# Four layers of sliding-window attention and Fourier mixing on one core: split weights kept in DRAM, residual rows loaded ahead, one late chunk regrouped, fill casts on GpSimd

## The chip, the core and the metric

The kernel runs on one core of a Trainium2 chip (trn2). The metric is the device time of one execution in microseconds (us); times given as a median are over several executions. Engines are named as the profile has them: PE (TensorE, the matmuls), PEld (its weight loads), DVE (VectorE), ACT (ScalarE), POOL (GpSimd), SP (SyncE, whose queue issues the DMAs).

## What is computed

The input `x` has S = 2048 rows of D = 640. Four layers run in a row, attention, Fourier, attention, Fourier, each as `x = x + layer(layernorm(x))`, with the same weights in both layers of a kind.

```python
def _A_ref(x, wqkv, wo):                       # H = 32 heads of Dh = 20, W = 256
    qkv = (lambda x, *d: x.transpose(*d))((x @ wqkv).reshape(B, S, 3, H, Dh), 2, 0, 3, 1, 4)
    q, k, v = qkv[0], qkv[1], qkv[2]
    scores = jnp.einsum("bhqd,bhkd->bhqk", q, k) * (Dh ** -0.5)
    mask = (idx[:, None] - idx[None, :] >= 0) & (idx[:, None] - idx[None, :] < W)
    scores = jnp.where(mask[None, None], scores, -1e9)
    o = jnp.einsum("bhqk,bhkd->bhqd", _softmax(scores, axis=-1), v)
    return o.transpose(0, 2, 1, 3).reshape(B, S, D) @ wo

def _B_ref(x, dft_seq_re, dft_seq_im, dft_hid_re, dft_hid_im):
    a = jnp.einsum("bsd,ed->bse", x, dft_hid_re)
    b = jnp.einsum("bsd,ed->bse", x, dft_hid_im)
    return jnp.einsum("ts,bse->bte", dft_seq_re, a) - jnp.einsum("ts,bse->bte", dft_seq_im, b)
```

## The kernel before

**Arithmetic.** Each fp32 operand of a large matmul is cut into two parts, hi (its cast to f32r) and lo (the operand minus hi), and each product is three matmuls (`product3`, L251; two half-array products at once in `lockstep`, L273). The cut is a cast on ACT and a subtraction on DVE or POOL (`split`, L242 and L248; as queued jobs `cut_job`, L235, and `sub_job`, L227, which halves a row tile on POOL).

**Stages of an attention layer** (`attention`, L372). `before_heads` normalises and transposes x and makes v and the first q/k chunks. `heads` (L631) has 8 quads of 4 heads and 16 steps a quad. A step makes a score block in one order (L656) and its row maximum on DVE (L661), sends the maxima, as `mt` (ACT, L672), by DMA into a row of `qp` (L674), makes the transposed scores with that row in the product (L684), takes the exponential on ACT (L694), masks it on POOL (L700, L704), and multiplies it with v (L719). So a row of maxima that is late holds L684 of the quad behind it. `after_heads` ends the layer, and interleaves its end with the start of the Fourier layer.

**What fills PE between the steps.** Three generators, taken up in this order by `fill`: `project` (L587) makes q/k chunks 2 to 9 of 128 columns, in sets of four 512-row blocks or, for the last two chunks, in the order `LAST` of two blocks each; `partials` (L1007) multiplies the first three of five 128-row chunks of the heads' output with `wo` and adds the residual rows (L1030); `late` (L1077) adds the last two chunks, the rest of the layer's output (L1117, L1123) and the next norm. A chunk is a regrouping of the 640 rows of the output by `CHUNKS` (rectangles of heads x columns), and each rectangle costs two DMAs, one of the output (L907) and one of the softmax denominators' reciprocals (L910). Scaling (L940; L923 after the heads) and the cut come behind them.

**What sets the order.** Engines run in the order of the program. [...] `tick` runs twice a step: it runs what was posted for now (`post`), takes one request for output chunks (`asks`) if a raw buffer is free (`room`), and takes one job from each of the lanes `act`, `dve` and `pool` (`job`).

**Weights before.** `load_chunk` (L514) loads a raw q/k weight chunk, `cut_chunk` (L520) cuts it by jobs on ACT and POOL, in both attention layers. `prepare(2)`, run at `LAST[2]`, asks for three raw `wo` chunks (`load_early`, L983), cut on ACT and DVE (key "ew"), beside the first output chunks; `poll_late` (L1055) loads the other two in the last quad, cut on POOL (key "lw"). `prepare(4)`, when `project` is at its end, loads the first four residual row blocks (L1005).

**A q/k result** is copied from PSUM by ACT (L563), cast on ACT (L571, a job of the lane `act`), subtracted on POOL in two jobs, and stored one tick later to `qk_d` (L542), from which `pack` loads the next quad's q and k (L619). **The late chunks** 3 and 4 both hold heads of the last quads; `late_load` (L1046) loads both, four rectangles or eight DMAs a block, when the last quad's part is stored.

## Time and profile before

| what | us |
|---|---|
| median of 3 runs (2234.83 to 2236.5) | 2236.22 |
| the profiled execution | 2236.0 |
| its span, first to last instruction | 2234.3 |
| PE busy | 2137.6 |
| DVE busy | 1605.3 |
| ACT busy | 1159.8 |
| POOL busy | 968.1 |

The profiled execution is 1.7 us longer than its span, and 0.2 us below the median. In rows of the timeline the columns are the start, the duration, the engine (SPq is SP's DMA issue), the line of the kernel and the operation, the tile written and the tiles read, and the count; in brackets stands the idle time of the engine before it and what ended it. Rows of groups have busy time, the mean in ns, and the idle time before. The two attention layers have their head stages at about 125 to 560 us and 1230 to 1660 us, and the Fourier layers lie between and behind. Such lines are quoted where the prediction uses them.

### The profile page before, as it was taken

Reading aid. Unit: us, or ns where it says so; the run is one execution under the profiler, and the core shown is the slowest. Engines: PE = TensorE matmul, PEld = TensorE weight load, DVE = VectorE, ACT = ScalarE, POOL = GpSimd, SP = SyncE. Lnnn points to the kernel's source line nnn. Section 1 sums busy time; section 2 is a strip of 40 time slices with the busy share of each in tenths; the row PEclk is TensorE's granted clock in tenths of the full one; section 3 lists DMA queues with packets and bytes.
Section 4 is the critical chain, followed back from the end, with each engine's and each line's share of the span. In section 5 each row is a group of like instructions: output and inputs, shape, how many; then the busy total and the mean of one; then the engine's idle time right before and its main releaser. Section 6 shows DMA issues by size and latency. Waiting matters only on the chain. (4 is left out here: it accounts for less than half of the span.)

```text
span 2234.3 us, 49112 instructions
## 1 busy us (share of the span) xinstructions
PE 2137.6 (96%) x17944; PEld 1787.5 (80%) x17944; DVE 1605.3 (72%) x3925; ACT 1159.8 (52%) x2161; POOL 968.1 (43%) x1572
## 2 busy tenths in 40 slices
PE   7999999898989999999999999998988999999999
PEld 7987777676868888889999777766777688888899
DVE  6357777685897868786661677776858978687776
ACT  2127776566554545452431477775665545455432
POOL 3036666775513223222330466667755132342324
PEclk9999999999999999999999999999999999999999
DMA  5545666774535354665646466667645354546653
GB/s 188 179 155 183 191 185 195 216 208 128 182 124 184 125 184 135 208 202 192 207 143 187 149 192 183 192 199 229 187 146 165 118 175 139 181 129 228 209 170 129
DMA packets 220498, 392.13 MB, mean 176 GB/s; under 512 B 39520, under 2 KB 86112, under 8 KB 220256
## 3 DMA queue, kind: packets, MB, share of 16 engines
q1 hardware_dynamic: 220256, 388.98, 55.3%
q8 instruction: 142, 2.33, 0.4%
q14 instruction: 100, 0.82, 0.1%
HBM read 273.94 MB, written 113.77 MB: 174 GB/s over the span
## 5 line engine op out<-in xcount | busy, mean ns | idle before, releaser
L661 DVE CUSTOM_DVE_ANT_0 banks<-banks,mask 128x384 f32<-128x384 f32 (+2 forms) x1024 | 527.8, 557 | 160.7 <-PE banks L656 135.5
L694 ACT ACTIVATE pt<-banks 128x768 f32<-128x768 f32 (+2 forms) x512 | 393.6, 770 | 177.2 <-PE banks L684 81.1
L700 POOL TENSOR_SCALAR_AFFINE_SELECT pt<-pt 128x256 f32<-128x256 f32 x512 | 210.8, 412 | 251.1 <-ACT pt L694 223.0
L273 PE MATMUL banks<-big,wc 64*128 64x512 f32 x1920 | 273.6, 396 | 0.4 <-DVE pt L459 0.4
L684 PE MATMUL banks<-qp,kp 61*128 61x384 f32 (+2 forms) x1024 | 209.9, 381 | 34.4 <-DVE mc L661 23.5
L656 PE MATMUL banks<-kp,qp 60*128 60x384 f32 (+2 forms) x1024 | 210.6, 351 | 11.4 <-ACT pt L694 10.5
L719 PE MATMUL banks<-pt,vq 128*32 128x128 f32 x5760 | 211.3, 278 | 1.6 <-ACT pt L694 1.6
L273 PEld LDWEIGHTS banks<-big,wc 64*128 64x128 f32 x1920 | 186.6, 186 | 25.0 <-ACT x L563 4.2
L684 PEld LDWEIGHTS banks<-qp,kp 61*128 61x128 f32 x1024 | 108.7, 185 | 97.4 <-DVE mc L661 62.1
L704 POOL TENSOR_SCALAR_AFFINE_SELECT pt<-pt 128x256 f32<-128x256 f32 x448 | 182.9, 408 | 0.0
L719 PEld LDWEIGHTS banks<-pt,vq 128*32 128x32 f32 x5760 | 142.2, 110 | 49.0 <-issue 36.1
L242 ACT ACTIVATE c<-pt 128x512 fp32r<-128x512 f32 x150 | 93.7, 626 | 160.8 <-POOL pt L1333 52.9
L242 ACT ACTIVATE qp<-pt 128x512 fp32r<-128x512 f32 (+1 forms) x195 | 119.8, 624 | 108.5 <-DVE pt L1347 51.0
L248 DVE TENSOR_TENSOR c<-pt,c 128x512 fp32r<-128x512 f32 x150 | 123.6, 826 | 54.6 <-ACT c L242 51.8
L656 PEld LDWEIGHTS banks<-kp,qp 60*128 60x128 f32 x1024 | 124.8, 187 | 44.0 <-ACT pt L694 27.1
L1413 PE MATMUL banks<-qp,big 128*128 128x512 f32 x630 | 154.5, 398 | 4.4 <-ACT qp L242 1.7
L248 DVE TENSOR_TENSOR qp<-pt,qp 128x512 fp32r<-128x512 f32 (+1 forms) x191 | 148.4, 785 | 12.6 <-ACT qp L242 9.9
L1346 POOL TENSOR_TENSOR pt<-pt,pt 128x512 f32<-128x512 f32 x34 | 50.3, 1481 | 236.3 <-DMA pt<-c 180.0
L661 DVE DVE_READ_ACCUMULATOR2_ANT mc<- 128x1 f32 x1024 | 145.2, 142 | 0.0
L1413 PEld LDWEIGHTS banks<-qp,big 128*128 128x128 f32 x630 | 120.3, 193 | 31.1 <-ACT qp L242 2.6
L1413 PE MATMUL banks<-qp,xc 128*128 128x512 f32 x480 | 117.3, 390 | 0.8 <-DVE xc L248 0.8
L227 POOL TENSOR_TENSOR c<-x,c 128x256 fp32r<-128x256 f32 x128 | 94.1, 741 | 44.1 <-ACT c L571 41.9
(240 smaller groups left out, 4474.3 us busy)
## 6 DMA issues: line engine op xcount, KB each, us to landing
pt<-c SPq DMA_DIRECT2D x188, 512.0 KB
qk_d<-c SPq DMA_DIRECT2D x80, 512.0 KB
kp<-qk_d SPq DMA_DIRECT2D x384, 80.0 KB
qp<-qk_d SPq DMA_DIRECT2D x384, 80.0 KB
kp<-u_d SPq DMA_DIRECT2D x32, 640.0 KB
o_d<-ou SPq DMA_DIRECT2D x64, 256.0 KB
x_d<-x SPq DMA_DIRECT2D x48, 320.0 KB
v_d<-pt SPq DMA_DIRECT2D x16, 768.0 KB
```

The lines of the kernel that those rows point to most:

```text
L227: eng.tensor_tensor(out=lo[..., c], in0=src[..., c], in1=hi[..., c].bitcast(F32), op=OP.subtract)
L242: nc.scalar.activation(hi, src, AF.Copy, scale=-1.0 if neg else 1.0)
L248: (eng or nc.vector).tensor_tensor(out=lo, in0=src, in1=hi.bitcast(F32), op=OP.subtract)
L273: self.nc.tensor.matmul(ps[a], x[r], y[r], start=half + i == 0, stop=half == 1 and i == n - 1, skip_group_check=True)
L656: nc.tensor.matmul(p, qp[quad % 2][b:b + 60, z, qb * P:(qb + 1) * P], kp[quad % 2][b:b + 60, z, k0 * P:(qb + 1) * P], start=True, stop=True)
L661: nc.vector.tensor_tensor_reduce(out=p, in0=p, in1=self.mask[:, 384 - n * P:], scale=1.0, scalar=NEG, op0=OP.add, op1=OP.max, accum_out=mc ...
L684: nc.tensor.matmul(self.banks[:, banks[e], :n * P], kp[quad % 2][b:b + 61, z, kb * P:(kb + 1) * P], qp[quad % 2][b:b + 61, z, kb * P:(kb + ...
L694: nc.scalar.activation(pt[quad, kb][:, 2 * z:2 * z + 2, :n * P], self.banks[:, b0:b1 + 1, :n * P], AF.Exp, scale=SCALE)
L700: nc.gpsimd.affine_select(out=t[:, :, 0:P], in_=t[:, :, 0:P], pattern=[[0, 2], [1, P]], compare_op=OP.is_ge, fill=0.0, base=0, channel_mul ...
L704: nc.gpsimd.affine_select(out=t[:, :, 256:384], in_=t[:, :, 256:384], pattern=[[0, 2], [-1, P]], compare_op=OP.is_gt, fill=0.0, base=0, ch ...
L719: nc.tensor.matmul(self.banks[32 * h:32 * h + 32, bank, :P], vq[:, 96 * (kb % 4) + 21 * h:96 * (kb % 4) + 21 * h + 32], t[:, h, (qb - kb) ...
L1413: nc.tensor.matmul(self.banks[:, bk, :], p, b[q], start=start and m == 0, stop=stop and last and m == 2, skip_group_check=True)
```

## The change

1. **q/k weights.** In the first attention layer a chunk is cut as before, and both parts are also stored to DRAM (`wq_d`, 640 KB a chunk). In the second (`fresh` is false) `cut_chunk` is one DMA of the parts into the tile, and there is no raw load, cast or subtraction.
2. **Output weights.** In the first layer `keep_wo` takes `wo` in ten halves of 320 columns, one every six steps: load, cast on ACT, subtraction on POOL, two stores to `wo_d`. Both layers then load parts: six DMAs of 320 KB in `prepare(2)`, four in `poll_late`. The cuts "ew" and "lw" go.
3. **Residual rows.** The 128-row blocks 0 and 1 are loaded into a tile of the weights' ring ("wc") at `LAST[3]`; `prepare(4)` loads blocks 2 and 3 only; the add of `partials` reads them from there.
4. **Late chunks.** Chunk 3 becomes heads 20 to 27, columns 0 to 15, one rectangle without a head of the last quad. Chunk 4 is heads 16 to 27, columns 16 to 19, and heads 28 to 31: two rectangles. The 512-row blocks 0 and 1 of chunk 3 are loaded at the start of the last quad (`late_first`) and worked on POOL while the heads run; its blocks 2 and 3, and chunk 4, stay after it.
5. **Casts of q/k results** move from ACT to POOL (`tensor_copy`, lane `pool`), the store comes three ticks after the subtraction instead of one, and `asks` wants one more free buffer. The last quad's reciprocals and their stores come a tick later.

The diff, without the helper arguments that follow from it:

```diff
 CHUNKS = (((0, 16, 0, 8),), ((0, 16, 8, 16),), ((0, 16, 16, 20), (16, 20, 0, 16)),
-          ((16, 20, 16, 20), (20, 28, 0, 14)), ((20, 28, 14, 20), (28, 32, 0, 20)))
+          ((20, 28, 0, 16),), ((16, 28, 16, 20), (28, 32, 0, 20)))
...
         self.od = dram.tile([H, 32, S], F32, name="o_d")
+        self.wod = dram.tile([2, KC, P, D], F32, name="wo_d")
+        self.wqd = dram.tile([NCH, P, 2 * D], F32, name="wq_d")
         self.rd = dram.tile([NSB, H, 512], F32, name="r_d")
...
         self.xn = {}
-        self.ready, self.hid = 0, False
+        self.ready, self.hid, self.fresh = 0, False, True
         self.slot = None
...
                 f()
-        if self.asks and self.room(2):
+        if self.asks and self.room(3):
             self.asks.popleft()()
...
     def load_chunk(self, c):
-        if c < NCH:
+        if c < NCH and self.fresh:
             raw, free = self.hold()
...
     def cut_chunk(self, c):
-        if c < NCH:
-            raw, free = self.turn.pop(("wraw", c))
-            w = self.work.tile([P, 2, KC, P], F32R, name="wc", tag="wc")
-            raw = raw.rearrange("p (k c) -> p k c", c=P)
-            self.turn["w", c] = w
-            if self.slot is None:
-                self.split(w[:, 0], w[:, 1], raw, eng=self.nc.gpsimd if c < 2 else None)
-                free()
-                return
-            for ks, done in ((slice(0, 3), None), (slice(3, KC), free)):
-                self.cut_job("pool", ("w", c), w[:, 0, ks], w[:, 1, ks], raw[:, ks], done)
+        if c >= NCH:
+            return
+        w = self.work.tile([P, 2, KC, P], F32R, name="wc", tag="wc")
+        self.turn["w", c] = w
+        flat = w.rearrange("p l k c -> p (l k c)").bitcast(F32)
+        if not self.fresh:
+            self.nc.sync.dma_start(flat, self.wqd[c])
+            return
+        raw, free = self.turn.pop(("wraw", c))
+        raw = raw.rearrange("p (k c) -> p k c", c=P)
...
+        def keep():
+            self.nc.sync.dma_start(self.wqd[c], flat)
+        if self.slot is None:
+            self.split(w[:, 0], w[:, 1], raw, eng=self.nc.gpsimd if c < 2 else None)
+            free()
+            keep()
+            return
...
+        def done():
+            free()
+            self.post(3, keep)
+        for ks, f in ((slice(0, 3), None), (slice(3, KC), done)):
+            self.cut_job("pool", ("w", c), w[:, 0, ks], w[:, 1, ks], raw[:, ks], f)
...
+    def keep_wo(self, i):
...
+        if i == 0:
+            self.wt = [self.slot_tile(f"rr{n}", 512, dt)[:, :320] for n, dt in enumerate((F32R, F32R, F32))]
+        if i == 2 * KC:
+            self.rr = [self.slot_tile(f"rr{n}", 512, F32) for n in range(3)]
+            return
+        k, cs = i // 2, slice(i % 2 * 320, i % 2 * 320 + 320)
+        hi, lo, raw = self.wt
+        self.nc.sync.dma_start(raw, self.a["wo"][:, k, cs])
...
+        def keep():
+            for n, t in enumerate((hi, lo)):
+                self.nc.sync.dma_start(self.wod[n, k, :, cs], t.bitcast(F32))
+        self.post(5, lambda: self.cut_job("pool", ("wo", i), hi, lo, raw, lambda: self.post(2, keep)))
...
                 if self.c_live == 3:
-                    self.post(1, lambda: self.job("act", key, lead))
+                    self.post(1, lambda: self.job("pool", key, lead))
                     return
...
                 st = self.work.tile([P, 2, 512], F32R, name="c", tag="c", bufs=3)
-                self.nc.scalar.activation(st[:, 0, :], r, AF.Copy)
-                self.sub_job("pool", key, st[:, 1, :], r, st[:, 0, :], lambda: (free(), self.post(1, lambda: store(st))))
+                self.nc.gpsimd.tensor_copy(st[:, 0, :], r)
+                self.sub_job("pool", key, st[:, 1, :], r, st[:, 0, :], lambda: (free(), self.post(3, lambda: store(st))))
...
                 self.packable.add((c, sb))
-            self.job("act", key, lead)
+            self.job("pool", key, lead)
         for r in self.lockstep(sets):
...
                 self.prepare(2)
+            if (c, sbs) == LAST[3]:
+                self.y_first = cuts(self.work.tile([P, 2 * D], F32, name="y", tag="wc"), D)
+                for t, y in enumerate(self.y_first):
+                    self.nc.sync.dma_start(y, self.xsrc[t * P:(t + 1) * P, :])
             yield from self.pieces(c, sbs, "m")
...
             cols = slice(bk * 512, (bk + 1) * 512)
-            at = (2, 9, 11) if quad < NQ - 1 else (1, 5, 6)
+            at = (2, 9, 11) if quad < NQ - 1 else (1, 6, 7)
             self.post(at[0], lambda: nc.sync.dma_start(sm, ou[0:P:32, :]))
...
                 f()
+            if self.fresh and step >= 0 and step % 6 == 2 and step // 6 <= 2 * KC:
+                self.keep_wo(step // 6)
             s, t, v = step + LEAD, step, step - 1
...
         key = "o", sb, k
-        lane, n, wait = ("pool", 2, 7) if k < EARLY else ("dve", 1, 4)
-        eng = nc.gpsimd if k < EARLY else nc.vector
+        busy = self.step + LEAD < 16 * NQ
+        lane, n = ("pool", 2) if busy else ("dve", 1)
+        wait = 7 if busy else 4
+        eng = nc.gpsimd if busy else nc.vector
...
             self.early_o = [dict(zip(ks, pairs(oc[:6]))), dict(zip(ks, pairs(oc[6:])))]
-            self.ask(0, self.load_early)
+            for k in ks:
+                self.load_wo(k, self.early_w[k])
+            self.ask(0)
             self.ask(1)
...
             self.take_big(2, F32)
-            self.load_y(range(AHEAD_X))
...
-    def load_early(self, k):
-        raw, free = self.hold()
-        self.nc.sync.dma_start(raw, self.a["wo"][:, k, :])
-        self.early_cut += 1
...
-        def cut():
-            self.early_cut -= 1
-            self.cut_job("dve", "ew", *self.early_w[k], raw, free)
-        self.post(4, cut)
...
-    def ask(self, sb, also=None):
+            self.load_y(range(2, AHEAD_X))
...
+    def load_wo(self, k, w):
+        for n in range(2):
+            self.nc.sync.dma_start(w[n].bitcast(F32), self.wod[n, k])
...
+    def ask(self, sb):
         o = self.early_o[sb % 2]
...
                 self.load_o(o, sb, k)
-            if also:
-                self.asks.append(lambda k=k: also(k))
             self.asks.append(one)
...
             assert b1 == b0 + 1
-            y = y.rearrange("p (f c) -> p f c", f=2)
-            nc.vector.tensor_tensor(out=y, in0=self.banks[:, b0:b0 + 2, :320], in1=y, op=OP.add)
+            x, y = [v.rearrange("p (f c) -> p f c", f=2) for v in (self.y_first[t] if t < 2 else y, y)]
+            nc.vector.tensor_tensor(out=y, in0=self.banks[:, b0:b0 + 2, :320], in1=x, op=OP.add)
             self.part_t = t + 1
...
         t = self.part_t
-        return t == NB or t % 4 or not (self.early_o[t // 4 % 2]["left"] or self.early_cut or
-                                        any("ew" == j[1] for q in self.lanes.values() for j in q))
+        return t == NB or t % 4 or not (self.early_o[t // 4 % 2]["left"])
...
+    def late_raws(self, sb):
+        p, c = [cuts(t, 512) for t in self.pt], self.late_c
+        return (cuts(c[2], 512), [c[0][:, :512], c[1][:, :512]], [p[0][2], p[1][2]], [p[2][2], None])[sb]
...
+    def late_first(self, sb):
+        o = self.late_pre[sb] = self.late_set(sb)
+        self.load_o(o, sb, EARLY, self.late_raws(sb)[0], self.vq[0] if sb == 3 else None)
...
     def late_load(self):
-        self.flush("lw")
         sb = len(self.late_o)
-        o = self.late_set(sb)
+        if sb not in self.late_pre:
+            self.late_first(sb)
+        o = self.late_pre[sb]
         self.late_o.append(o)
-        p, c = [cuts(t, 512) for t in self.pt], self.late_c
-        raws = (cuts(c[2], 512), [c[0][:, :512], c[1][:, :512]], [p[0][2], p[1][2]], [p[2][2], None])[sb]
-        for k in range(EARLY, KC):
-            self.load_o(o, sb, k, raws[k - EARLY], self.vq[k - EARLY] if sb == 3 else None)
+        self.load_o(o, sb, EARLY + 1, self.late_raws(sb)[1], self.vq[1] if sb == 3 else None)
...
             for k in range(EARLY, KC):
-                raw = self.late_c[k - EARLY][:, :D]
-                self.nc.sync.dma_start(raw, self.a["wo"][:, k, :])
-                self.post(4, lambda k=k, raw=raw: self.cut_job("pool", "lw", *self.late_w[k - EARLY], raw))
+                self.load_wo(k, self.late_w[k - EARLY])
+        if n in (1, 4):
+            self.late_first(n // 4)
         if n == 4:
...
         self.hid = True
+        self.fresh = False
```

6 lines of the change are left out of this document (2 added, 4 removed).

## The prediction

> **What bounds the kernel now.** I read the head of the page first, then the list of what TensorE waited for, then each long wait in the timeline. Columns of the page: busy us, share of the span, instructions.
>
> ```profile
> span 2234.3 us, 49112 instructions
> PE 2137.6 (96%) x17944; PEld 1787.5 (80%) x17944; DVE 1605.3 (72%) x3925; ACT 1159.8 (52%) x2161; POOL 968.1 (43%) x1572
> ```
>
> TensorE (PE) is busy 96% of the span, so the idle time left in the whole kernel is 2234.3 − 2137.6 = 96.7 us. The change leaves the order of instructions on PE as it is: each of its matmuls stays, in the same place. All that it can win is idle time of PE and the slow clock that follows idle time. Next, what ended those waits (us in total, times, longest):
>
> ```profile
> PE banks L684 <- DVE mc L661: 23.5, 39, 5.0
> PE banks L656 <- ACT pt L694: 10.5, 27, 1.3
> PE banks L255 <- DVE x L1123: 7.2, 4, 3.7
> PE banks L255 <- DVE kp L227: 6.6, 2, 3.4
> PE banks L684 <- DMA qp<-mt: 5.8, 2, 3.0
> ```
>
> A few long waits carry most of it. The timeline of PE has them one by one, four in each attention layer (start, duration; in brackets the idle time before it and what ended it):
>
> ```profile
> 419.72 0.44 PE L684 MATMUL banks<-qp,kp 61*128 61x384 f32 x2 [2.78 <-DMA qp<-mt]
> 438.37 0.58 PE L684 MATMUL banks<-qp,kp 61*128 61x256 f32 x2 [4.61 <-DVE mc L661]
> 556.29 0.56 PE L255 MATMUL banks<-qp,kp 128*128 128x320 f32 x2 [3.37 <-DVE kp L227]
> 574.50 0.56 PE L255 MATMUL banks<-qp,kp 128*128 128x320 f32 x1 [2.24 <-DVE x L1123]
> ...
> 1527.05 0.69 PE L684 MATMUL banks<-qp,kp 61*128 61x384 f32 x2 [3.04 <-DMA qp<-mt]
> 1545.85 0.58 PE L684 MATMUL banks<-qp,kp 61*128 61x256 f32 x2 [4.96 <-DVE mc L661]
> 1663.46 0.90 PE L255 MATMUL banks<-qp,kp 128*128 128x320 f32 x2 [3.22 <-DVE kp L227]
> 1683.02 0.85 PE L255 MATMUL banks<-qp,kp 128*128 128x320 f32 x4 [3.71 <-DVE x L1123]
> ```
>
> I call the four kinds, in this order, the **mt**, **y**, **late 1** and **late 2** stall. They sum to 13.0 + 14.93 = 27.9 us. They cost more than their own length. Stretches behind two of them, and one of the undisturbed head stage (stretch, length, then busy us of PE, PEld, DVE, ACT, POOL, granted PE clock, DMA share, GB/s):
>
> ```profile
> 574.70:578.00 3.30, 3.30 (x13) 3.30 (x14) 2.96 (x9) 0.96 (x3) 1.93 (x2) 0.50 0.90 274
> 1544.00:1550.80 6.80, 4.95 (x42) 4.35 (x46) 4.26 (x14) 1.19 (x2) 1.63 (x4) 0.50 0.87 271
> ...
> 206.00:262.00 56.00, 54.17 (x750) 40.15 (x746) 44.57 (x167) 42.72 (x78) 35.66 (x86) 1.00 0.58 180
> ```
>
> After a stall PE runs at clock 0.50 for some 3.3 us, or 6.8 us after the longest. A stretch that is full of matmuls at half clock loses half its length: 3.3/2 = 1.65 us, and 4.95/2 = 2.5 us of the long one. I count 1.65 for each stall but that one. So eight stalls hold 27.9 + 7 × 1.65 + 2.5 = 42 us, 1.9% of the span: the most that the change can win from them. In the undisturbed head stage PE has 54.17 of 56 us; little is to be had there.
>
> [...]
>
> **The change, part by part.**
>
> *Residual rows ahead (y).* How the vector engine and the queue of SyncE stand at the stall:
>
> ```profile
> 1540.24 2.27 SPq L1005 DMA_DIRECT2D big<-x_d  x5
> ```
>
> ```profile
> 1539.44 0.14 DVE L661 DVE_READ_ACCUMULATOR2_ANT mc<- 128x1 f32 x1
> 1544.44 0.82 DVE L1030 TENSOR_TENSOR big<-banks,big 128x640 f32<-128x640 f32 x1 [4.86 <-DMA big<-x_d]
> 1553.16 0.82 DVE L1030 TENSOR_TENSOR big<-banks,big 128x640 f32<-128x640 f32 x1 [0.20 <-PE banks L684]
> ```
>
> DVE stands 4.86 us at L1030 for a load that was issued at 1540.24 only; the row maxima that PE needs stand behind it. The changed kernel loads rows 0 and 1 one filler earlier, into a tile that is free when the filler LAST[2] ends, and L1030 reads them there. Rows 2 and 3 keep the old place, but the second L1030 came 8.7 us after the first, and the third is again later, while the load took 4.2 us. So this stall goes whole: 4.61 + 4.96 + 1.65 + 2.5 = **−13.7 us**. What is late next on DVE is a matmul result (0.20 us above). Two more 320 KB DMAs stand earlier on SyncE's queue; that is in the mt term.
>
> *One late chunk out of the last quad (late 1, late 2).*
>
> ```profile
> 1648.16 0.66 SPq L907 DMA_DIRECT2D cr<-o_d  x1
> ...
> 1653.58 0.76 SPq L910 DMA_DIRECT2D rr<-r_d  x1
> ...
> 1671.08 0.67 SPq L910 DMA_DIRECT2D rr<-r_d  x1
> ...
> 1673.72 1.37 SPq L910 DMA_DIRECT2D rr<-r_d  x1
> ```
>
> ```profile
> 1658.12 1.30 DVE L940 TENSOR_TENSOR cr<-cr,rr 128x512 f32<-128x512 f32 x2 [0.34 <-DMA r_d<-rc]
> ...
> 1662.72 1.28 DVE L227 TENSOR_TENSOR kp<-cr,kp 128x512 fp32r<-128x512 f32 x2
> ```
>
> ```profile
> 569.65 0.69 DVE L923 TENSOR_TENSOR pt<-pt,rr 128x512 f32<-128x512 f32 x1 [2.15 <-DMA rr<-r_d]
> ...
> 1676.29 0.69 DVE L923 TENSOR_TENSOR pt<-pt,rr 128x512 f32<-128x512 f32 x1 [2.34 <-DMA rr<-r_d]
> 1678.18 0.69 DVE L923 TENSOR_TENSOR pt<-pt,rr 128x512 f32<-128x512 f32 x1 [1.19 <-DMA rr<-r_d]
> ```
>
> Late 1: eight small DMAs, two scales (1.30 us) and two subtractions (1.28 us) after the last quad become four DMAs, one scale and one subtraction. The subtraction stays behind the same residual adds and norm statistics on DVE, from 1659.33 to 1662.72. So the DMAs that are gone win nothing; one scale less wins 1.30/2 = 0.65 us, and PE can do chunk 3 while it waits for chunk 4, which I put at as much again, from the 0.90 us of the first two matmuls. I take −1.4 us in each layer, **−2.8 us**; ends −1.3 (the scales alone) and −3.37 − 3.22 − 3.3 = −9.9 (the stall gone with its clock). A gap of about 2 us remains and I take no clock back for it.
>
> Late 2: the scales at L923 hold DVE 2.15 us in layer 1, 2.34 + 1.19 = 3.53 us in layer 2, and the L1123 adds for which PE waits (2.24 and 3.71 us) stand behind them. Eight small DMAs become six, so that the last is issued where the sixth stood, 1673.72 − 1671.08 = 2.64 us earlier. In layer 1 that covers the 2.15, in layer 2 2.64 of 3.53. With the clock of layer 1 alone: −2.15 − 2.64 − 1.65 = **−6.4 us**; ends 0 (the landing, not the issue, is what is late: the large transfers share the time) and −2.24 − 3.71 − 3.3 = −9.3.
>
> *Weights' parts by DMA (mt).* Three rows of SyncE's queue, and the ScalarE instruction that makes mt:
>
> ```profile
> 1516.10 0.25 ACT L672 ACTIVATE mt<-banks 16x128 fp32r<-16x128 f32 x1
> ```
>
> ```profile
> 1518.81 0.37 SPq L542 DMA_DIRECT2D qk_d<-c  x1
> 1519.31 0.57 SPq L907 DMA_DIRECT2D x<-o_d  x1
> 1522.26 1.06 SPq L619 DMA_DIRECT2D kp<-qk_d  x3
> ...
> 1523.91 1.31 SPq L674 DMA_DIRECT2D qp<-mt  x2
> ```
>
> mt was ready at 1516.35 and issued at 1523.91, because SyncE's queue was full and stood 2.4 us from 1519.9 to 1522.26 for the store of 1518.81 to land. Six loads of wo parts (320 KB) in one burst take the place of three raw loads there, two residual loads come in and two o loads move behind: by the programs' order 66 DMAs instead of 62 up to this mt, but more of them early. From the rows above, a small one costs some 0.5 us, so 4 more are 2 us; but the cutting of wo on DVE, and the wait for the raw buffers, are gone. Either the store is issued earlier and the stall goes, −2.78 − 3.04 − 3.3 = −9.1; or GpSimd, with the casts, brings that store later, and it stays or grows by 2 us in each layer, +4. I take the middle of "stays" and "goes", **−4.6 us**.
>
> *Casts on GpSimd, and the first layer's extra stores.* Group rows (count | busy us, mean ns):
>
> ```profile
> L571 ACT ACTIVATE c<-x 128x512 fp32r<-128x512 f32 x64 | 40.3, 636 | 5.0 <-DMA qk_d<-c 4.2
> ```
>
> ```profile
> L484 POOL CAST mask<-x 128x384 bf16<-128x384 f32 x1 | 0.5, 498 | 0.0
> L227 POOL TENSOR_TENSOR c<-x,c 128x256 fp32r<-128x256 f32 x128 | 94.1, 741 | 44.1 <-ACT c L571 41.9
> L1333 POOL TENSOR_TENSOR pt<-pt 128x512 f32<-128x512 f32 x30 | 43.1, 1439 | 74.2 <-DMA pt<-c 54.4 <-DVE c L248 8.8 <-DVE qp L248 4.5
> ```
>
> ACT loses 64 × 0.636 = 40.7 us. No PE wait names that line, and the waits on ACT's exp (L694) are 10.5 us in 27 pieces; I book nothing, with −6 as the far end. POOL gains 64 casts of 512 columns. No such row exists: one input of 384 columns took 0.498, so 512 take some 0.498 × 512/384 = 0.66 us; the two-input form took 1.439. I take 0.66, nearest in kind. 32 casts in eight 56 us windows are 4 × 0.66 = 2.7 us more on 35.66, and keeping wo adds at most 2 × 0.741 us for each of ten halves, about 15 us over four windows: 42 of 56 us. PE's list names no wait on POOL in the heads, so this hides behind its idle time, except where POOL is dense already (before the y stall). I take **+2 us** for that, and **+1 us** for the stores of wq parts that stand ahead of loads at the start; ends 0 and +10 for the two.
>
> [...]
>
> **Sum.** −13.7 − 2.8 − 6.4 − 4.6 + 3 = −24.5 us on the profiled execution's 2236.0 us (span 2234.3 and 1.7 around it): 2211.5. That execution lies 0.2 us under the median of the runs shown, 2236.22, which is nothing against their spread; I say **2212**.
>
> **The rivals.**
>
> *Queue full (2217).* SyncE's queue is the limit before the last quads, and six loads in a burst keep mt late. For it: the queue issued back to back there. Against it: two of its waits go. Then the mt term is 0 to +4 instead of −4.6: 2216 to 2221.
>
> *The late chunk is not the late thing (2219).* DVE's own order, or the landing of the 512 KB transfers, sets late 1 and late 2. For it: L227 keeps its place on DVE. Then −2.8 − 6.4 falls to −1.3: 2212 + 7.9 = 2220.
>
> *All goes (2201).* Also the rest of mt (−4.5), late 2 (−2.9) and some of the ACT waits (−4): 2212 − 11 = 2201.
>
> *Slower: a load that blocks SyncE.* In the second layer a chunk of wq is one 640 KB DMA into the tile of the chunk two before, and it stands on SyncE's in-order queue until PE has done with that tile; masks, q, k and v loads queue behind it. In the trace mt was issued 7.6 us late and cost 3.0 us of PE, so about 4.6 us of delay are free. Seven chunks that each block 9 us would cost 7 × (4.4 + 1.65) = 42 us: 2212 + 42 = 2254. It outweighs the gains from 24.5/7 = 3.5 us a chunk with the clock, which is a blocking of some 6.5 us. Against it: the program issues that load only behind the fillers that read the tile.
>
> **How the numbers follow.** Forecast 2205 to 2216: 0.42. Queue full: 0.15. Late chunk not the late thing: 0.12. All goes, 2195 to 2205: 0.14. Gains given back by queue and GpSimd, within 0.2%: 0.05. Slower: 0.12. A measurement of this kernel can tell about 0.2% (4.5 us) from no change. Faster 0.42 + 0.15 + 0.12 + 0.14 = 0.83, same 0.05, slower 0.12. The range: 2197 leaves out 0.04 below; 2233 leaves out the slower cases and most of the equal ones, 0.16.
>
> **What would show it.** y right: no wait of DVE on residual loads at L1030, and no PE gap of 4 to 5 us near 438 and 1546. Late 2 right: L923 waits under 1 us. Late 1 right: the gap at L255 behind L227 is still there, at 1.5 to 2 us. mt: its row of issue against L672. GpSimd: the cast's mean is 0.6 to 0.8 us, and PE's list names no wait on POOL in the heads. Wrong would be: a new long gap of PE in the head stages of either layer, a clock under 1.00 there, or SyncE standing for wc in the second layer.

## The result and the profile after

The changed kernel takes 2227.95 us (median of 15 runs, 2220.09 to 2233.69) against 2235.27 us before (15 runs, 2228.42 to 2236.67): ratio 0.9971, 95% interval 0.9959 to 0.9982, some 7 us faster. The forecast was 2212 us, 24 us faster; the direction held, the size was under a third of it. The head of the page after, and what PE waited for (us in total, times, longest). Lines have moved: L684 is now L719, L656 is L691, L694 is L729, L661 is L696.

```profile
span 2226.4 us, 48984 instructions
PE 2127.7 (96%) x17944; PEld 1791.7 (80%) x17944; DVE 1597.3 (72%) x3910; ACT 1115.6 (50%) x2080; POOL 999.4 (45%) x1648
```

```profile
PE banks L719 <- DMA qp<-mt: 16.5, 5, 5.1
PE banks L719 <- DVE mc L696: 13.6, 34, 1.3
PE banks L691 <- ACT pt L729: 10.1, 6, 4.4
...
PE banks L257 <- DVE x L1159: 6.3, 4, 2.8
PE banks L257 <- DVE kp L229: 5.0, 2, 2.5
```

The row of the y stall (DVE mc, 23.5 us with a longest of 5.0) has lost its long waits. The mt row has grown from 5.8 to 16.5 us. PE's idle time as a whole is 2226.4 − 2127.7 = 98.7 us, 2 us more than before; what fell is PE's *busy* time, by 9.9 us, with the same instructions and a granted clock that was lower in the mean (0.987 against 0.991). The long waits one by one, in the timeline of PE:

```profile
295.13 0.44 PE L691 MATMUL banks<-kp,qp 60*128 60x384 f32 x1 [2.64 <-ACT pt L729]
...
332.23 0.69 PE L691 MATMUL banks<-kp,qp 60*128 60x384 f32 x1 [4.37 <-ACT pt L729]
...
402.07 0.69 PE L719 MATMUL banks<-qp,kp 61*128 61x384 f32 x2 [4.64 <-DMA qp<-mt]
...
558.65 0.57 PE L257 MATMUL banks<-qp,kp 128*128 128x320 f32 x2 [2.49 <-DVE kp L229]
...
575.56 0.71 PE L257 MATMUL banks<-qp,kp 128*128 128x320 f32 x3 [2.26 <-DVE x L1159]
...
1498.02 0.69 PE L719 MATMUL banks<-qp,kp 61*128 61x384 f32 x2 [5.13 <-DMA qp<-mt]
...
1565.32 0.69 PE L719 MATMUL banks<-qp,kp 61*128 61x384 f32 x2 [3.98 <-DMA qp<-mt]
...
1656.38 0.85 PE L257 MATMUL banks<-qp,kp 128*128 128x320 f32 x4 [2.50 <-DVE kp L229]
...
1673.34 0.90 PE L257 MATMUL banks<-qp,kp 128*128 128x320 f32 x2 [2.83 <-DVE x L1159]
```

Two waits in the first layer's heads are new (295 and 332 us). They stand for the exponential, and ACT's timeline shows what held that: the cast of a wo half, which `keep_wo` puts on ACT, stands for its load, or for the store of the half before.

```profile
294.34 0.47 ACT L237 ACTIVATE rr<-rr 128x320 fp32r<-128x320 f32 x1 [3.00 <-DMA rr<-wo]
...
331.00 0.47 ACT L237 ACTIVATE rr<-rr 128x320 fp32r<-128x320 f32 x1 [4.36 <-DMA wo_d<-rr]
```

The 5.13 us wait at 1498 (and its twin at 402) comes behind the burst of wo parts. First SyncE's queue, then DVE:

```profile
1477.24 2.79 SPq L1024 DMA_DIRECT2D big<-wo_d  x6
...
1485.44 0.61 SPq L771 DMA_DIRECT2D sm<-ou  x1
...
1493.84 1.16 SPq L709 DMA_DIRECT2D qp<-mt  x2
```

```profile
1491.27 0.25 DVE L774 RECIPROCAL rc<-sm 128x16 f32<-128x16 f32 x1 [2.48 <-DMA sm<-ou]
```

An 8 KB load issued at 1485.44 lets DVE go on at 1491.27, 5.8 us later, and mt, made at 1483.85, is issued at 1493.84. Whether the burst makes that lag is tried below (wo_spread). Put together, PE by the number of its instruction (its order is the same in both kernels, but for some neighbours that change places): at the 10,000th the changed kernel is 0.7 us behind, at the 13,000th, still in the second layer's heads, 8.4 us ahead, at the 13,500th 5.7 us ahead, and so it stays, 8 us at the end. So the first layer won nothing, and the second layer's *steady* heads, which the prediction booked at nothing, won 9 us. That it came out faster at all was luck: act_casts, below, shows that without that gain nothing is left.

### The profile page after: what moved, and what is told of

Its sections match the earlier page's. It is cut to its first block, busy times and chain, and to the rows that moved or that the text cites. A ratio compares the mean times of both kernels' runs of the same rounds, so it can differ in the third digit from the quotient of the medians.

```text
span 2226.4 us, 48984 instructions
## 1 busy us (share of the span) xinstructions
PE 2127.7 (96%) x17944; PEld 1791.7 (80%) x17944; DVE 1597.3 (72%) x3910; ACT 1115.6 (50%) x2080; POOL 999.4 (45%) x1648
## 4 chain that ended last, share of the span: by engine, by line
PE 76%; DVE 7%; DMA 6%; POOL 3%; ACT 3%; issue 3%; SPq 2%; ACTq 0%; DVEq 0%; POOLq 0%
PE banks L1449 29%; PE banks L257 15%; PE banks L275 12%; PE banks L754 6%; PE banks L719 5%; PE banks L1738 4%; PE banks L691 4%; ACT pt L729 1%; DMA qp<-mt 1%; DMA qp<-qk_d 1%; DVE banks L696 1%; DMA x<-o_d 1%; DMA kp<-qk_d 1%; DVE qp L250 1%; DVE big L1062 1%
## 5 line engine op out<-in xcount | busy, mean ns | idle before, releaser
L696 DVE CUSTOM_DVE_ANT_0 banks<-banks,mask 128x384 f32<-128x384 f32 (+2 forms) x1024 | 528.1, 557 | 164.2 <-PE banks L691 140.1
L729 ACT ACTIVATE pt<-banks 128x768 f32<-128x768 f32 (+2 forms) x512 | 394.2, 771 | 199.0 <-PE banks L719 85.9
L719 PE MATMUL banks<-qp,kp 61*128 61x384 f32 (+2 forms) x1024 | 210.3, 382 | 33.4 <-DMA qp<-mt 16.5
L691 PE MATMUL banks<-kp,qp 60*128 60x384 f32 (+2 forms) x1024 | 205.8, 345 | 14.3 <-ACT pt L729 10.1
L719 PEld LDWEIGHTS banks<-qp,kp 61*128 61x128 f32 x1024 | 108.6, 185 | 96.4 <-DVE mc L696 56.1
L250 DVE TENSOR_TENSOR qp<-pt,qp 128x512 fp32r<-128x512 f32 (+1 forms) x191 | 155.1, 819 | 12.2 <-ACT qp L244 9.5
L691 PEld LDWEIGHTS banks<-kp,qp 60*128 60x128 f32 x1024 | 125.2, 188 | 34.7 <-ACT pt L729 13.9
L696 DVE DVE_READ_ACCUMULATOR2_ANT mc<- 128x1 f32 x1024 | 145.2, 142 | 0.0
L1449 PEld LDWEIGHTS banks<-qp,xc 128*128 128x128 f32 x480 | 89.9, 188 | 20.2 <-DVE xc L250 1.6
```

The source lines that it names most:

```text
L250: (eng or nc.vector).tensor_tensor(out=lo, in0=src, in1=hi.bitcast(F32), op=OP.subtract)
L691: nc.tensor.matmul(p, qp[quad % 2][b:b + 60, z, qb * P:(qb + 1) * P], kp[quad % 2][b:b + 60, z, k0 * P:(qb + 1) * P], start=True, stop=True)
L696: nc.vector.tensor_tensor_reduce(out=p, in0=p, in1=self.mask[:, 384 - n * P:], scale=1.0, scalar=NEG, op0=OP.add, op1=OP.max, accum_out=mc ...
L719: nc.tensor.matmul(self.banks[:, banks[e], :n * P], kp[quad % 2][b:b + 61, z, kb * P:(kb + 1) * P], qp[quad % 2][b:b + 61, z, kb * P:(kb + ...
L729: nc.scalar.activation(pt[quad, kb][:, 2 * z:2 * z + 2, :n * P], self.banks[:, b0:b1 + 1, :n * P], AF.Exp, scale=SCALE)
L1449: nc.tensor.matmul(self.banks[:, bk, :], p, b[q], start=start and m == 0, stop=stop and last and m == 2, skip_group_check=True)
```

## The experiments

The median is over the executions of that kernel; the ratio is to the kernel before on the same chip, with its 95% interval. "Parts" are those of the list in the section on the change.

| run | kernel | median us | ratio |
|---|---|---|---|
| - | changed: parts 1 to 5 | 2227.95 | 0.9971 (0.9959 to 0.9982) |
| y_only | part 3 alone | 2231.13 | 0.9979 (0.9963 to 0.9996) |
| cast_only | part 5 alone | 2217.39 | 0.9920 (0.9906 to 0.9934) |
| act_casts | changed, without part 5 | 2236.49 | 1.0006 (0.9990 to 1.0022) |
| no_wo | changed, without part 2 | 2219.20 | 0.9918 (0.9904 to 0.9933) |
| no_wo_wq | parts 3, 4, 5 | 2221.48 | 0.9946 (0.9925 to 0.9966) |
| no_wo_chunk | parts 1, 3, 5 | 2218.26 | 0.9932 (0.9919 to 0.9944) |
| wo_spread | changed, wo parts asked for two at a time | 2223.74 | 0.9939 (0.9924 to 0.9954) |
| keep8b | changed, wo halves cast later | 2221.88 | 0.9949 (0.9935 to 0.9962) |
| mt_act | changed, mt's DMAs from ACT's queue | 2335.93 | 1.0465 (1.0431 to 1.0498) |
| no_wo_mt | no_wo, mt's DMAs from ACT's queue | 2330.41 | 1.0426 (1.0391 to 1.0462) |
| y_pack | y_only, q/k loads a step later | 2231.91 | 0.9987 (0.9971 to 1.0004) |
| before_pack | before, q/k loads a step later | 2236.67 | 1.0009 (0.9992 to 1.0025) |
| after_pack | changed, q/k loads a step later | 2235.29 | 1.0008 (0.9994 to 1.0023) |
| no_wo_pack | no_wo, q/k loads a step later | 2223.22 | 0.9947 (0.9932 to 0.9963) |
| half_before | before, half as many q/k loads | 2258.19 | 1.0112 (1.0096 to 1.0128) |
| y_half | y_only, half as many q/k loads | 2264.06 | 1.0140 (1.0111 to 1.0170) |
| after_half | changed, half as many q/k loads | 2263.23 | 1.0143 (1.0114 to 1.0173) |
| no_wo_half | no_wo, half as many q/k loads | 2233.30 | 0.9983 (0.9962 to 1.0004) |

**The rows ahead, alone (y_only).** The edit is part 3 of the diff on the kernel before:

```diff
+            if (c, sbs) == LAST[3]:
+                self.y_first = cuts(self.work.tile([P, 2 * D], F32, name="y", tag="wc"), D)
...
-            self.load_y(range(AHEAD_X))
+            self.load_y(range(2, AHEAD_X))
```

> The kernel before with one part of the change: residual rows 0 and 1 loaded ahead (part 3). In the changed kernel the 4.6 and 5.0 us stalls behind L1030 are gone, but waits of PE for mt grew from 5.8 to 16.5 us. Theory A, the parts are independent and this one does what was forecast: some 12 us faster than before (ratio 0.9945, 2223 us), with mt waits of 5.8 us as before. Rival B, the end of the y stall brings the next row of maxima up against a queue that is as late as before: 4 to 6 us faster only, mt waits of 9 us or more.

It won 4.7 us (0.9 to 8.3), rival B. PE's two longest waits in the second layer are now waits for mt:

```profile
1527.71 0.69 PE L688 MATMUL banks<-qp,kp 61*128 61x384 f32 x2 [4.89 <-DMA qp<-mt]
...
1572.49 0.45 PE L688 MATMUL banks<-qp,kp 61*128 61x384 f32 x2 [3.08 <-DMA qp<-mt]
```

SyncE's rows of mt in that stretch, first of the kernel before, then of y_only:

```profile
1536.18 1.16 SPq L674 DMA_DIRECT2D qp<-mt  x2
...
1551.99 1.15 SPq L674 DMA_DIRECT2D qp<-mt  x2
```

```profile
1525.01 1.23 SPq L678 DMA_DIRECT2D qp<-mt  x2
...
1536.18 1.16 SPq L678 DMA_DIRECT2D qp<-mt  x2
...
1552.55 1.15 SPq L678 DMA_DIRECT2D qp<-mt  x2
```

The reader is to see that the y stall is gone and the next two rows of maxima leave at the same times as before. The stall on the residual rows lay on top of a queue that was as late as it: the 4.96 us had been hiding waits for mt, 1.07 and 3.08 us behind the stall's place. The wait ahead of it, 3.04 us before, grew to 4.89: its mt was made 1.2 us earlier and issued 1.1 us later, and the two residual loads now stand ahead of it on SyncE's queue, at 1511.49. By PE's instruction numbers the rows won 1.4 us in the first layer's heads and none in the second's; of the 4.9 us that the profiled execution gained, 3.3 lie behind the second layer's heads, where this edit was not priced.

**Part 2 undone (no_wo).** `load_early`, its cuts "ew" and "lw", and the raw loads come back; `keep_wo` goes:

```diff
-            for k in ks:
-                self.load_wo(k, self.early_w[k])
-            self.ask(0)
+            self.ask(0, self.load_early)
...
-            if self.fresh and step >= 0 and step % 6 == 2 and step // 6 <= 2 * KC:
-                self.keep_wo(step // 6)
```

> The changed kernel with part 2 undone: wo is loaded raw and cut in both layers as before (the 512-row block 1 of late chunk 3 two steps later, for its buffer). Theory A, the gain went to part 2: PE waits of 2.64 and 4.37 us at 295 and 332 us (the cast of a wo half stands on ACT until a DMA lands) go with their slow clock, about 8 us, and the mt waits of 4.64 and 5.13 us at 402 and 1498 us behind the burst of six 320 KB loads shrink to 3 us or less, about 6 us: 2214 us, ratio to before 0.9905. Rival B, the casts on GpSimd bring the stores late and that makes the waits: the mt waits stay at 12 us or more in sum, 2221 to 2226 us.

2219.2 us: part 2 costs 0.9971 − 0.9918 = 0.5%, 12 us, the larger part of what was expected. The mt waits fall from 16.5 to 4.6 us, theory A. At the last transposed score product of the second layer's heads this kernel is 24 us ahead of the kernel before, though with 81 fewer filler matmuls behind it, and at the end of the span 17 us. Part is given back where the Fourier layer begins, where PE, there early, waits for its operands. PE's waits of that place in the first layer:

```profile
PE banks L1443 <- ACT qp L243: 4.8, 1, 4.8
PE banks L1443 <- DVE qp L249: 3.5, 1, 3.5
```

**The burst spread (wo_spread).** Two loads of wo parts are put ahead of each request for an output chunk:

```diff
-            for k in ks:
-                self.load_wo(k, self.early_w[k])
-            self.ask(0)
+            self.ask(0, lambda k: self.load_wo(k, self.early_w[k]))
```

> The changed kernel with the six loads of wo parts asked for two at a time between the requests for output chunks, instead of in one burst. Theory A, the burst is what makes the denominators' load (5.8 us to landing) and mt late: DVE's 2.5 us wait for it and the mt waits of 4.64 and 5.13 us at 402 and 1498 us go down to 2 us or less, 8 to 10 us faster than the changed kernel, 2219 us. Rival B, the queue is too full at any spacing: the same waits move by a few us and the time stays within 2 us of the changed kernel's 2228.

2223.7 us, 4 us better than the changed kernel by the medians and 7 by the ratios, between the two theories. DVE no longer waits for sm there, but PE's mt waits of 4.49 us at 403 and 5.08 us at 1499 us remain (20.1 us in all). So the burst explains DVE's wait, not PE's. Of the two waits on the exponential in the first layer's heads, on which this edit has no bearing, one is gone here and one is 4.14 us: what single executions show of these waits scatters.

**The wo halves cast later (keep8b).** The raw half goes into an x buffer, the halves start at step 0 and not 2:

```diff
-        self.post(5, lambda: self.cut_job("pool", ("wo", i), ...
+        self.post(8, lambda: self.cut_job("pool", ("wo", i), ...
```

> The changed kernel with the cast of each wo half eight ticks after its load instead of five, the halves starting two steps earlier and loaded into a free x buffer. Theory A, ACT stands at that cast for the load or for the store of the half before (3.0 and 4.4 us ahead of PE's waits of 2.64 and 4.37 us): these two waits go, with the slow clock 7 to 9 us, 2220 us; the second layer stays as it is. Rival B, what waits is only moved, since SyncE's queue is behind in the first layer: waits of PE of 2 us or more appear elsewhere between 170 and 390 us, 2226 to 2229 us.

2221.9 us, 5 to 6 us better than the changed kernel, somewhat less than theory A gave. Between 224 and 392 us the waits on the exponential fell from 9.5 to 0.2 us, while mt waits (4.2 us) and a wait for row maxima (3.0 us) came up: theory A in the main, with a piece of rival B. With the halves every eight steps and the cast nine ticks after the load, still in the old tile (keep_later), the kernel deadlocks, so that form has no time.

**mt from ACT's queue (mt_act, no_wo_mt).** One word in `m_rows`:

```diff
-                self.post(1, lambda z=z: nc.sync.dma_start(
+                self.post(1, lambda z=z: nc.scalar.dma_start(
```

> The changed kernel with the two small DMAs of each row of maxima (mt, L709) issued from ScalarE's queue instead of SyncE's. Theory A, mt is late because it stands in SyncE's order behind loads that wait for a q/k store to land (lags of 6 to 11 us from ACT's mt to the issue) and behind large transfers of the same ring: PE's mt waits fall from 16.5 us to under 4 us, with the slow clock 14 to 18 us, 2212 us. Rival B, the 16 DMA engines are full, or the q and k loads on SyncE's queue are as late as mt: waits of PE for qp, kp, sm or mt of 10 us or more remain, 2221 to 2226 us.

> Part 2 undone (wo raw and cut in both layers) and mt issued from ScalarE's queue. Theory A, what part 2 costs and what SyncE's order costs are separate: beside 2219.2 us for part 2 undone alone, its last mt waits (4.6 us) and the DVE waits behind the same queue go, 2212 to 2214 us, the fastest kernel so far. Rival B, without the wo parts the queue is no longer what is late and nothing is won: 2218 to 2220 us.

Both far slower. PE's list for mt_act has no mt row among its seven longest any more. That alone does not show that SyncE's queue had held mt, since PE itself runs late here. Issuing a pair takes ACT 1.07 us, and the exponential stands behind it. ACT's timeline, and the first row of PE's list:

```profile
1359.70 1.07 ACTq L709 DMA_DIRECT2D qp<-mt  x2
1360.90 1.51 ACT L729 ACTIVATE pt<-banks 128x768 f32<-128x768 f32 x2 [1.23 <-PE banks L691]
```

```profile
PE banks L691 <- ACT pt L729: 66.8, 57, 7.8
```

Against the changed kernel the 64 pairs cost 110 us by the ratios (1.0465 − 0.9971), 1.7 us each, for 1.07 us of ACT. This was the sign of what the prediction had missed: in a head step, ACT is on PE's path.

**The casts (act_casts, cast_only).** Part 5 undone on the changed kernel (the casts' engine and the store's tick; the free buffer and the last quad's reciprocals stay), and part 5 alone on the kernel before. Of the first edit, the cast:

```diff
-                self.nc.scalar.activation(st[:, 0, :], r, AF.Copy)
+                self.nc.gpsimd.tensor_copy(st[:, 0, :], r)
```

> The changed kernel with part 5 undone: the casts of q/k results on ACT again, the store one tick after the subtraction. In the changed kernel a quad of the second layer takes 43.4 us instead of 44.8, which the prediction booked at nothing. Theory A, that gain is the casts' leaving ACT: a quad goes back to 44.8 us, the time grows by 8 to 12 us to some 2238 us. Rival B, it is the cuts of wq that left the second layer (part 1): a quad stays at 43.4 us there, and the first layer, where GpSimd's lane held the wo subtractions 6 us, gets faster: 2222 to 2226 us.

> The kernel before with part 5 alone: the casts of q/k results on GpSimd, the store three ticks after the subtraction, the last quad's reciprocals a tick later. In the changed kernel a quad of the second layer's steady heads is 1.7 us shorter, and the casts put back on ACT cost 8.5 us. Theory A, ACT's exponential is on the path of each head step (an mt pair on ACT, 1.07 us, cost PE about as much), so the casts' leaving is worth 1.4 to 1.7 us a quad in both layers and this part alone is 12 to 18 us faster than before: 2216 to 2222 us. Rival B, the gain shows only where the wq cuts are gone too: 2228 to 2234 us.

Theory A in both. Without the casts' move the other four parts are worth nothing (1.0006); the move alone is worth 0.8%, 18 us (15 to 21), more than twice the whole change. The steady heads show it layer by layer. From the first transposed score product (L684) of a layer to the 256th behind it, four quads in which no output chunk is asked for yet, the kernels differ from the kernel before by (us in the first and in the second layer, minus is faster, one execution each):

| run | first layer | second layer |
|---|---|---|
| cast_only | −7.2 | −7.0 |
| no_wo | −6.6 | −7.3 |
| no_wo_wq | −7.2 | −7.1 |
| changed | +7.3 | −7.0 |
| wo_spread | +10.0 | −7.5 |
| keep8b | +3.8 | −7.3 |
| act_casts | +9.6 | −0.2 |
| y_only | −0.1 | +0.2 |

Each kernel with the casts on GpSimd gains 7 us where no wo half is cut, and each kernel that cuts wo halves loses it and more in the first layer. With the cast the store's tick moves too, here and in act_casts, and no run parts the two. That it is the cast is read from ACT's timeline. How a cast stood in the way, in ACT's timeline of the kernel before:

```profile
1345.23 0.81 ACT L694 ACTIVATE pt<-banks 128x768 f32<-128x768 f32 x1
1346.02 0.60 ACT L563 ACTIVATE x<-banks 128x512 f32<-128x512 f32 x1
1346.65 0.63 ACT L571 ACTIVATE c<-x 128x512 fp32r<-128x512 f32 x1
1347.18 0.79 ACT L694 ACTIVATE pt<-banks 128x768 f32<-128x768 f32 x1
1347.88 0.59 ACT L563 ACTIVATE x<-banks 128x512 f32<-128x512 f32 x1
1348.35 0.28 ACT L726 ACTIVATE ou<-banks 128x128 f32<-128x128 f32 x1
1348.51 0.65 ACT L571 ACTIVATE c<-x 128x512 fp32r<-128x512 f32 x1
1349.03 1.76 ACT L694 ACTIVATE pt<-banks 128x768 f32<-128x768 f32 x2
```

From 1345.23 to 1350.8 ACT has no gap, and the exponentials, which free the banks for the next score block, stand behind a copy and a cast each. The steady 56 us from 1328 us (us of PE first, instructions in brackets), of before, of the changed kernel and of cast_only:

```profile
1328.00:1384.00 56.00, 54.91 (x797) 41.50 (x789) 43.19 (x170) 42.09 (x77) 39.77 (x92) 1.00 0.63 192
```

```profile
1328.00:1384.00 56.00, 55.65 (x809) 42.87 (x807) 44.82 (x177) 40.31 (x72) 39.34 (x94) 1.00 0.68 210
```

```profile
1328.00:1384.00 56.00, 55.64 (x803) 42.78 (x803) 46.15 (x174) 41.34 (x76) 41.94 (x99) 1.00 0.66 199
```

PE's busy time in these 56 us is 0.7 us longer, and it gets through its instructions faster than that: from its 10,000th to its 13,000th it took 221.4 us before and 212.3 in the changed kernel. Of these 9.1 us, 3.8 are idle time (5.2 to 1.4 us); the rest is in the matmuls themselves, which the profile calls busy: from start to start, without the idle time, the 314 of L684 in that stretch took 40.4 us, then 36.2, and the 314 of L656 41.7, then 40.9. That the profile counts part of a wait as busy is read from this; no run shows it by itself. The score block of 1272 to 1484 us (count | busy us, mean ns | idle before), before and changed:

```profile
L656 PE MATMUL banks<-kp,qp 60*128 60x384 f32 x262 | 55.4, 364 | 3.8 <-ACT pt L694 3.6
```

```profile
L691 PE MATMUL banks<-kp,qp 60*128 60x384 f32 x274 | 55.8, 354 | 0.0
```

The price on GpSimd was as forecast: the cast took 614 ns in cast_only (forecast 0.66 us), and no long wait of PE in that kernel names POOL.

```profile
L571 POOL CAST c<-x 128x512 fp32r<-128x512 f32 x64 | 39.1, 614 | 37.3 <-ACT x L563 35.3 <-DMA qk_d<-c 2.0
```

And in cast_only the y stall is gone without part 3. What DVE's residual add waited for, in the kernel before and in cast_only:

```profile
its engine sat idle before it (us, times) until:
...
  DMA big<-x_d: 4.9, 1
  DMA big<-x: 4.5, 1
...
```

```profile
its engine sat idle before it (us, times) until:
  PE banks L273: 23.9, 21
  PE banks L684: 2.8, 7
```

No DMA is in it, where before 4.9 and 4.5 us were. Its stores, requests and fillers come in another order (it has 36 matmuls fewer); that the residual rows are there in time for this reason is not shown.

**What the other parts are worth (no_wo_wq, no_wo_chunk).** On no_wo, `load_chunk` and `cut_chunk` as before; or `CHUNKS`, `late_load` and the lane choice in `load_o` as before.

> Parts 3, 4 and 5: as no_wo (2219.2 us), and the q/k weights loaded raw and cut in both layers as before. Theory A, part 1 takes seven casts and fourteen subtractions from the second layer's heads, off PE's path, and adds stores to the first: 2217 to 2221 us, the same as no_wo. Rival B, the cuts of wq on ACT cost PE as much as the casts of q/k results do (7 times 0.94 us in the second layer): 2223 to 2226 us.

> Parts 1, 3 and 5: as no_wo (2219.2 us), with the late chunks grouped, loaded and cut as before. In no_wo the heads end earlier and PE waits 8.2 us a layer where the Fourier layer begins. Theory A, part 4 shortens the attention's end by the 2 to 4 us a layer that late 1 and late 2 lost in the changed kernel: without it 2222 to 2226 us. Rival B, the end is set by the last quad's chain whatever the chunks are: 2217 to 2221 us.

Without part 1 0.9946, without part 4 0.9932, with both 0.9918. So part 1 is worth some 0.3% beside the others, part 4 some 0.1%, and the intervals overlap. For part 4 that is rival B: its medians, 2218.3 and 2219.2 us, are the same. For part 1 it stays open whether it is worth something: in the four quads of the table above, where it takes the cuts out of the second layer, no_wo_wq and no_wo are alike. Beside part 5, parts 1, 3 and 4 together are worth nothing that can be told: cast_only has 0.9920, no_wo 0.9918.

**Loads moved behind mt (y_pack, before_pack, after_pack, no_wo_pack).** I took it that mt was late behind the q/k loads that wait for a store to land. One edit in `heads`:

```diff
-                    defer(i // 3, f)
+                    defer(i // 3 + 1, f)
```

> The kernel before with residual rows 0 and 1 loaded ahead, and every group of q and k loads for the next quad issued one step later, so that the loads that wait for the last q/k store stand behind the mt of that step instead of ahead of it. With the rows alone the y stall went and the mt waits grew from 5.8 to 16.0 us (2231.1 us). Theory A, mt is late because it stands in SyncE's order behind a load that waits for a store's landing (1518.54 to 1523.37 us): the mt waits fall to 6 us or less, and the gain of the rows shows: 2220 to 2223 us. Rival B, the queue is behind by the number of its DMAs: mt is as late as with the rows alone, 2229 to 2232 us.

> The kernel before with only the q and k loads one step later. Theory A: the mt waits of 2.8 and 3.0 us go, the y stalls of 4.6 and 5.0 us stay, 6 to 9 us faster than before, 2227 us. Rival B (the queue's length holds mt): 2233 to 2236 us. Rival C, the y stall takes over what the mt stall gives, as the mt stall did for the y stall: y waits of 7 us, 2234 us.

> The changed kernel with the q and k loads one step later. Theory A: the mt waits behind the y stall's old place (3.98 us at 1565 us, 1.95 at 469) go; those behind the burst of wo parts (4.64 and 5.13 us at 402 and 1498) stay, since the burst and not a store holds the queue there: 4 to 6 us faster than the changed kernel, 2222 to 2224 us. Rival B: 2227 to 2229 us. If the burst's waits go too, the burst did not make them: 2214 us.

> Part 2 undone and the q and k loads one step later. Without part 2 the time was 2219.2 us with mt waits of 4.6 us and waits for row maxima (L675) of 10.4 us in the last quads, and 8.2 us of waits where the Fourier layer starts. Theory A: the mt and row maxima waits halve, but the attention's end gives back part, since the heads end earlier and wait for the last quad's chunks: 2214 to 2217 us. Rival B: 2218 to 2220 us.

Theory A fell. y_pack is no faster than y_only; its mt waits are 11.9 us, and the mt that had been issued at 1525.01 is issued at 1524.50, though a group of loads now stands behind it. after_pack and no_wo_pack are 6 to 8 us slower than without the edit, before_pack is the same within its interval. In the first four quads of either layer the edit costs these kernels some 1.6 us (4.0 in the first layer of after_pack); where the rest comes from was not followed up.

**Half as many q/k loads (y_half, half_before, after_half, no_wo_half).** `pack` takes two 512-column blocks at once, when the first is due:

```diff
-                for i, f in enumerate(self.pack(q, j)):
+                for i, f in enumerate(self.pack(q, j, True) if j % 2 == 0 else ()):
```

> The kernel before with residual rows 0 and 1 loaded ahead, and the q and k loads of a quad made for two 512-column blocks at once: half as many DMAs (48 a quad instead of 96), the same bytes, the same order of the rest. Loading the rows alone left the mt issues of that stretch where they had been (1536.18 us in both, 1551.99 and 1552.55 us after it), and moving loads behind mt won nothing. Theory C, SyncE's queue sets the pace there by the number of its DMAs (48 in 28 us, at 0.43 us each and the gaps between them): mt waits fall from 16.0 us to 4 us or less, and the y gain shows: 2217 to 2222 us. Rival D, the bytes or the landing times hold it, not the number: mt waits of 10 us or more, 2228 to 2232 us.

> The kernel before with half as many q and k loads, and nothing of the change. Theory C: the mt waits (5.8 us) go, the y stalls get no shorter than 4 us, since the residual loads wait for the fillers' end as before: 2227 to 2230 us. Rival D: 2233 to 2236 us. If y_half is faster than this by 9 us or more, loading the rows ahead is worth what was forecast once the queue is free.

> The changed kernel with half as many q and k loads. Theory C: its mt waits (16.5 us) fall to 6 us or less, and the waits on the wo halves' cast in the first layer (7.0 us) shrink, since their loads and stores are issued earlier: 2208 to 2214 us. If only the burst of wo parts is the limit, the waits near 400 and 1498 us stay at 4 us or more: 2218 to 2222 us. Rival D: 2226 to 2229 us.

> Part 2 undone and half as many q and k loads. Theory C: the heads get faster by the mt and row maxima waits (15 us in sum before), but the attention's end, where PE waits 8 us a layer for the last quad's chunks when the heads end early, gives half back: 2208 to 2214 us, against 2219.2 us for part 2 undone alone. Rival D: 2217 to 2220 us.

All are slower, by 14 us and more against the same kernel without the edit. The queue did get shorter, from 48 to some 32 DMAs in 28 us, and mt stayed late. PE's list for y_half:

```profile
PE banks L690 <- DMA qp<-mt: 14.7, 7, 4.0
PE banks L662 <- ACT pt L700: 13.4, 26, 3.4
PE banks L662 <- DVE mc L667: 13.1, 8, 3.5
```

So the number of q/k loads alone does not hold mt, and theory C fell. The edit is not clean either: a load of two blocks wants both blocks' results early, which puts their casts and copies on ACT at once. PE's waits at L662 for row maxima are new (0.2 us in y_only), and those for the exponential are longer (9.8 us there, the longest 1.2). **What holds SyncE's queue in the last quads stays open.** no_wo and cast_only, whose fillers stand in another order, have mt waits of 4.6 and 3.8 us only. What remains are large transfers and their landing: in y_only, from 1536 to 1570 us, SyncE itself waited 4.4 us for residual loads (320 KB) to land. This was not tried by itself.

## Why the prediction was wrong

The step of the prediction that failed is its bound: it let the change win only the idle time that PE's list names, and so booked the casts at nothing and of part 2 little more than GpSimd's share. The runs showed −18 us for the casts alone and +12 us for part 2, and −4.7 us instead of −13.7 for the rows ahead. Two of its own signs of being wrong came: new long gaps in the head stages (4.37 us before 332.23), and the clock of 0.50 behind them.

- **The bound.** "All that it can win is idle time of PE and the slow clock that follows": wrong. PE's busy time fell 9.9 us with the same instructions; it seems that a score matmul that waits is in part counted as busy (364 against 354 ns). The longest single waits were a poor guide: they hold 28 us, and the largest gain lay in the steady heads, where from 1272 to 1484 us PE's list names 3.6 us of waits on the exponential, none over 0.5 us.
- **Casts: "I book nothing, with −6 as the far end".** The argument was that PE's list names only 10.5 us of waits on the exponential and no wait on L571. Measured alone −18 us. The 0.66 us was right (614 ns), and no wait of PE on POOL came; the price of +2 us itself was not measured.
- **y: "So this stall goes whole", −13.7.** The stall went, the gain did not: −4.7 alone. The prediction named a matmul result as what is late next on DVE, and put SyncE into another term; what was late next was SyncE's mt, in the same stretch.
- **mt: −4.6, the middle.** It went the other way: PE's mt waits grew by 10.7 us. Of the two outcomes that I bounded ("goes", −9.1; "grows by 2 us in each layer", +4) the bad one was still too small. The rival "queue full" (2217, 0.15) had the direction. Its reason, the burst of six loads, held for DVE's wait alone (wo_spread); what else holds mt stays open.
- **wo in the first layer: "about 15 us over four windows", hidden on GpSimd.** Only GpSimd's share was priced. The cast of each half stands on ACT in order, and waits for a DMA; I did not name who is queued behind it. It cost waits of 2.64 and 4.37 us of PE, and behind the second the clock stood at 0.50 (332.30 to 335.60 us). The four quads with the halves in them lost 7.3 us in the first layer where they gained 7.0 in the second, so some 14 us went there. Part 2 as a whole cost 12 us.
- **Late 1: −2.8.** The gaps went from 3.37 and 3.22 to 2.49 and 2.50 us, −1.6, no clock back, as said (granted clock 0.91 from 550 to 590 us and from 1650 to 1690 us, in both kernels), at about half the size. **Late 2: −6.4.** 2.24 to 2.26 and 3.71 to 2.83: −0.9. DVE's waits at the scales did fall under 1 us, as the sign asked, but the work between them and L1159 did not, and by no_wo_chunk part 4 is worth little or nothing.
- **The slower rival** did not come: no wait of PE in the second layer stands behind a chunk load. The range held the time (2197 to 2233, measured 2227.95), by the rivals that it took in.

No run here has the cast of the q/k results on DVE. Against ACT, this cast took 614 ns on GpSimd (cast_only) and 636 on ACT (the kernel before), and moving it won 0.8%: what counted was whose path it left.

## A faster version

cast_only, one part of the five, takes 2217.39 us, 0.9920 (0.9906 to 0.9934) of the kernel before; no_wo, four parts, 0.9918 (0.9904 to 0.9933). They can't be told apart, both beat the changed kernel's 0.9971, and cast_only is the smaller edit.

## What to carry to other kernels

Before a stall is priced as a gain, look for the next late thing on *every* queue of that stretch, and compare issue times: a transfer that leaves at the same time with and without the stall will take its place (here the mt at 1536.18 us, in the kernel before and in y_only). An engine at half load can still be on the path, if its instructions stand in order between two that the busiest engine waits for (ACT was busy 52% of the span before, and the casts' leaving it won 18 us): look at the order in its timeline, and price the work moved off it by its place. An instruction put on such an engine should not wait for a DMA: here ACT stood 3.00 and 4.36 us at a cast, and PE 2.64 and 4.37 us behind it.

## What was not expected of the hardware

Issuing one DMA from ACT's queue took it 0.5 us (1.07 us a pair), and cost more on the path than that (1.7 us a pair by the ratios). The clock at 0.50 followed the idle gap of 2.26 us before 575.56 us here too, as a gap of 2.24 us did before the change; but behind the longer gaps of 2.50 us (before 1656.38) and 2.64 us (before 295.13) it stayed at 1.00. So the length of a gap alone does not say whether the clock falls. Two stretches of the changed kernel (columns as in the prediction, the granted clock third from the end):

```profile
577.00:580.00 3.00, 3.00 (x10) 2.52 (x10) 2.98 (x8) 1.74 (x4) 0.94 (x2) 0.50 0.96 252
...
1656.40:1659.80 3.40, 3.40 (x17) 2.80 (x17) 2.52 (x8) 0.30 (x1) 1.31 (x2) 1.00 0.80 248
```

An 8 KB load issued some 5 us behind the six wo parts took 5.8 us from issue to the instruction that waited for it. Most of the parts had landed by then: SyncE itself stood for them, 3.3 us in all between 1474 and 1498 us.
